# Twenty-one identity products on TensorE in the first tiles, and SyncE's DMA instructions in the order of the listing

## The chip, the cores and the metric

The kernel runs on one core of a Trainium2 chip. Its time is the device time of one execution in microseconds (us). Three executions of the kernel before took 613.67, 614.55 and 615.40 us; the median is 614.55 us.

## What is computed

Attention with a mask from hashed buckets, followed by a gated convolution block. There are 4 batches of 8 heads; each (batch, head) has 768 rows of 64 numbers. Cut to what matters:

```python
q_bits = (np.einsum('bhsd,dk->bhsk', q, proj) > 0)      # 6 sign bits of each row
k_bits = (np.einsum('bhsd,dk->bhsk', k, proj) > 0)
mask = q_bucket[:, :, :, None] == k_bucket[:, :, None, :]
scores = np.where(mask, scale * q @ k.T, -1e9)
attn = softmax(scores)                                  # rows of 768
x = attn @ v                                            # heads side by side: (4, 768, 512)
gate = sigmoid(causal convolution of x over 5 rows, weights conv_w)
out = (gate * (x @ w_val)) @ w_out
```

## The kernel before

**Units and tiles.** A unit is one (batch, head): 32 of them, numbered 0 to 31. A tile is 128 query rows of a unit: 6 per unit, 192 in all, numbered `k`. The main loop runs over `k`. For each tile TensorE makes the scores (`s`, four products, L311), VectorE the row maxima (`nm`, L317) and two small factors (the last is `nb`, L327), ScalarE the exponentials (`p`, L335), GpSimd the division by the row sums (L351), TensorE six transposes (`tp`, L360), ScalarE the copies of them (`pt`, L369). When all six tiles of a unit are transposed, `attn_v` multiplies by the values (`av`, L383) in six steps, two in every iteration with odd `k`. The convolution and the two large products (`pair_x`, `moe`, L445 and L470) are generators that get a step per iteration too, so that they fill TensorE between the tiles of later units. Their results leave through `out_dram<-o` (L480).

**What a unit needs before its first scores.** `prep(i)` prepares unit `i` while unit `i-1` is worked on. It begins in the iteration that starts the scores of unit `i-1` (L562), and goes on one step per iteration (L575). In the order of the listing it
- loads the values `vt` (L181; only for even units, since one load serves two heads). `vt` has two buffers, so the load for unit `i` can't start before `attn_v(i-3)` has read the older buffer for the last time;
- rounds the raw rows `r` to `aq` (GpSimd, L197), and, a step later, makes the remainder `bq` (GpSimd, L200);
- copies halves of them between partitions with four DMAs: `ak<-aq` (L201), `bk<-aq` (L202), `bk<-bq` (L203), `bq<-aq` (L204). The fourth overwrites what the third reads, so it waits until the third has landed;
- puts the bucket rows behind them with two small DMAs, `aq<-u` (L210) and `ak<-u` (L211); for later units they come out of DRAM and are named `ud`;
- loads the raw rows of unit `i+5` (`load_raw`, L212, the DMA is L175).

The scores of unit `i` read `aq`, `ak`, `bq`, `bk`, so they wait for the last of these six DMAs.

**The bucket rows.** `bits(i)` makes them for four units at once, from the raw rows of units `i` to `i+3`: a product of four parts (`m<-r`, L217) and a comparison (L222). The table `marks` (L537) says in which iteration a step runs: for units 8 to 11 the first product is in iteration 34, for units 12 to 15 in iteration 58. The raw rows of unit 11 are loaded by `prep(6)`, those of unit 15 by `prep(10)`. For units 16 and later `early_bits` does the same from rows loaded into `hh` and `hl` (L240).

**The start.** `first_prep` prepares unit 0 without DMAs between partitions. Its product `tp<-r,proj_sb` (L277) and the comparisons from it (L288) come first, then the scores of tile 0. `first_bits` makes the bucket rows of units 0 to 3 by two products L217 in the first iterations.

**What sets the order.** The work is listed under `tc.manual_schedule(engines=ENGINES)` (L522): on each engine in `ENGINES` the instructions stand in the order of the listing. Before, the set holds TensorE (PE), ScalarE (ACT), VectorE (DVE) and GpSimd (POOL). SyncE (SP) is not in it: a scheduler with a cost model set the order of its instructions. SP issues all DMAs but one, and does nothing else. It takes them strictly one after the other: if the next one has to wait for an engine or for a DMA, all behind it stand too.

Of the kernel before, what the change touches and what calls it, by code (L numbers as in the profile page):

```python
# [8 lines left out]
FP32 = mybir.dt.float32  # L9
# [6 lines left out]
I32 = mybir.dt.int32  # L16
U32 = mybir.dt.uint32

ENGINES = {mybir.EngineType.PE, mybir.EngineType.Activation, mybir.EngineType.DVE, mybir.EngineType.Pool}
BIG = float(2.0 ** 60)  # L20
TINY = float(2.0 ** -126)

# [4 lines left out]
def kernel(  # L27
# [10 lines left out]
    nc = tc.nc  # L38
    B, H, _, S = qk.shape
    P = 128  # L40
# [27 lines left out]
    ps_v = ctx.enter_context(tc.tile_pool(name="ps_v", bufs=1, space=PSUM))  # L68
    ps_m = ctx.enter_context(tc.tile_pool(name="ps_m", bufs=1, space=PSUM))

    ident = const.tile([P, P], FP32, name="ident")
# [65 lines left out]
    def load_conv():  # L137
        if conv_w.dtype == mybir.dt.int64:
            w = const.tile([P, NP * KW, 2], I32, name="cw64")
            nc.sync.dma_start(out=w, in_=conv_w.bitcast(I32).rearrange("p (n t) -> p n t", t=2))  # L140
            t = const.tile([P, NP * KW], FP32, name="cwt")
            yield
            a, d = yield from from_float64(w, t)
            yield
            nc.vector.tensor_tensor(out=cw_sb, in0=d, in1=a, op=ALU.add)
        else:
            nc.sync.dma_start(out=cw_sb, in_=conv_w)

    def load_weights():
        parts = [(src[:, c, :], hl[0][:, c, :], hl[1][:, c, :])  # L150
                 for src, hl in ((w_val, wv), (w_out, wo)) for c in range(NP)]
        here = []

        def fetch():
            if len(here) == len(parts):
                return
            src = parts[len(here)][0]
            if src.dtype == mybir.dt.int64:
                w = wst.tile([P, 512, 2], I32, name="w64")
                nc.sync.dma_start(out=w, in_=src.bitcast(I32).rearrange("p (n t) -> p n t", t=2))  # L160
            else:
                w = wst.tile([P, 512], FP32, name="w32")
                nc.sync.dma_start(out=w, in_=src)
            here.append(w)

        fetch()
        for n, (_, hi, lo) in enumerate(parts):
            yield
            yield from split_weight(here[n], hi, lo, fetch)

    def load_raw(i):
        if i < len(units):
            b, h = units[i]
            raws[i] = raw.tile([P, S], FP32, name="r")
            nc.sync.dma_start(out=raws[i], in_=qk[b, h])  # L175

    def load_values(i):
        b, h = units[i]
        if h % 2 == 0:
            vts[i] = vp.tile([P, KB, P], FP32, name="vt")  # L180
            nc.sync.dma_start(out=vts[i], in_=v[b, h // 2])  # L181
        else:
            vts[i] = vts[i - 1]
# [78 lines left out]
    def first_bits():  # L262
        u = stk.tile([P, S], FP32R, name="u", bufs=2)
        for hf in range(2):
            yield
            sl = slice(hf * HS, (hf + 1) * HS)
            signs(u[:, sl], product([raws[jj][:, sl] for jj in range(4)]))
        cur["u"] = u
        load_raw(5)

    def first_prep():

        r = raws[0]
        aq, ak, bq, bk = stacks[0] = [stk.tile([P, S], FP32R, name=nm) for nm in ("aq", "ak", "bq", "bk")]
        z = ps_t.tile([P, 512], FP32, name="tp")
        for g in range(4):
            nc.tensor.matmul(out=z[32 * g:32 * g + 2 * NB, 0:HS], lhsT=proj_sb[:, 2 * NB * (g // 2):2 * NB * (g // 2 + 1)],  # L277
                             rhs=r[:, HS * (g % 2):HS * (g % 2 + 1)], start=True, stop=True, tile_position=(0, 32 * g))
        nc.scalar.copy(out=aq[0:D], in_=r[0:D])
        nc.vector.tensor_copy(out=bk[D:P], in_=r[D:P])  # L280
        nc.vector.tensor_copy(out=ak[0:D], in_=r[D:P])
        nc.gpsimd.tensor_tensor(out=bk[0:D], in0=r[D:P], in1=bk[D:P].bitcast(FP32), op=ALU.subtract)

        def low_part(o, e):
            nc.vector.tensor_tensor(out=bq[D:P, o:e], in0=r[0:D, o:e], in1=aq[0:D, o:e].bitcast(FP32), op=ALU.subtract)  # L285

        def one_hot(g, o, e):
            nc.vector.tensor_scalar(out=(aq, ak)[g // 2][D:M, HS * (g % 2) + o:HS * (g % 2) + e],  # L288
                                    in0=z[32 * g:32 * g + 2 * NB, o:e],
                                    scalar1=rows_sb[32 * g:32 * g + 2 * NB, 2:3],  # L290
                                    scalar2=rows_sb[32 * g:32 * g + 2 * NB, 3:4], op0=ALU.is_ge, op1=ALU.mult)

        one_hot(0, 0, P)
        one_hot(2, 0, HS)
        one_hot(3, 0, HS)
        low_part(0, P)
        one_hot(0, P, HS)
        low_part(P, HS)
        nc.scalar.copy(out=bq[0:D], in_=r[0:D])
        yield  # L300
        one_hot(1, 0, HS)
        low_part(HS, S)

    def scores(k):
        i, qt = tiles[k]
        aq, ak, bq, bk = stacks[i]
        qs = slice(qt * P, (qt + 1) * P)
        s = ss[k] = ps_s.tile([P, 2, 512], FP32, name="s")
        for lq, rk, n in ((aq, ak, M), (bq, bk, P)):
            for hf in range(2):  # L310
                nc.tensor.matmul(out=s[:, hf, 0:HS], lhsT=lq[0:n, qs],  # L311
                                 rhs=rk[0:n, hf * HS:(hf + 1) * HS], start=n == M, stop=n == P)
# [195 lines left out]
    def step(gens):  # L508

        while gens:  # L510
            try:
                return next(gens[0])
            except StopIteration:
                gens.pop(0)
# [6 lines left out]
    N = len(tiles)  # L521
    with tc.manual_schedule(engines=ENGINES):  # L522
        for i in range(5):
            load_raw(i)
        load_values(0)
        rest = first_prep()
        next(rest)
        weights = [[load_weights()], [load_conv()]]
        preps = [first_bits(), prep(1)]
        scores(0)  # L530
        next(preps[1])
        step(preps)
        step(weights[0])
        step(weights[1])
        ahead = [early_bits()]
        near = {i: [bits(i)] for i in (4, 8, 12)}
        marks = {10: near[4], 11: ahead, 16: near[4], 17: ahead, 22: ahead, 28: ahead, 34: near[8], 40: near[8], 46: ahead, 52: ahead,  # L537
                 54: ahead, 56: ahead, 58: near[12], 60: near[12], 62: ahead, 64: ahead}
        for gens in near.values():
            step(gens)  # L540
        for k in range(N + LAG + 1):
            if 0 <= k - LAG - 1:
                keep_transposed(k - LAG - 1)
            pair = k % 2 == 0 and 0 <= k - 2 < N
            if k < N:
                maxima(k)
            if pair:
                row_sums(k - 2)
            if k < N:
                factors(k)  # L550
            if pair:
                recip(k - 2)
            if 0 <= k - 2 < N:
                normalise(k - 2)
            if k < N:
                shifts(k)
            if k == 0:
                finish([rest])
            if k + 1 < N:
                if tiles[k + 1][0] != tiles[k][0]:  # L560
                    finish(preps)
                    preps = [prep(tiles[k + 1][0] + 1)]  # L562
                scores(k + 1)
            if k < N:
                exponentials(k)
            if k - 1 in marks and k - 1 not in (11, 17):
                step(marks[k - 1])
            if k >= 60 or k % 2:
                step(convs)

            thin = k // 6 % 8 in (7, 0) and k < 186
            for _ in range(3 if cur["gates"] else (1, 0)[k % 2] if thin else 1):
                step(moes)
            cur["gates"] = max(0, cur["gates"] - 1)
            step(preps)  # L575
            if k in marks:
                step(marks[k])
            if k in (3, 7, 9, 13, 15):
                step(weights[1])
            if k % 6 != 3 and k > 4:  # L580
                step(weights[0])
            if k % 2:
                step(avs)
                step(avs)
            if 0 <= k - LAG < N:
                transposes(k - LAG)
        accs[:] = [(ps_m, "m"), (ps_t, "tp"), (ps_s, "s"), (ps_t, "tp"), (ps_s, "s")]
        finish(avs)
        cur["gates"] = 0
        cur["end"] = True  # L590
        while convs:
            step(convs)
            step(moes)
        finish(moes)
# [59 lines left out]
```

## Time and profile before

| | |
|---|---|
| median of three executions | 614.55 us (613.67 to 615.40) |
| the profiled execution's own time | 613.79 us |
| its span, first to last instruction | 611.9 us |
| PE busy (matmuls, ends modelled) | 585.5 us, 96% of the span |
| DVE, ACT, POOL busy | 428.8, 420.2, 386.5 us (70%, 69%, 63%) |
| DMA queue of SP | 28832 packets, 63.93 MB, 38.1% of 16 engines' span |

A row of the timeline has start and duration in us, the engine, the line, the operation, the tile written and the tiles read, and how many instructions it stands for; in brackets how long the engine was idle before, and what ended that. `SPq` rows are DMA issues: their duration is the time of issuing, not of the transfer. A row of the waits has the waiting engine and line, what it waited for, then the total in us, how often, and the longest.

### The profile page before, as it was taken

How to read it: one execution, taken by the hardware profiler on the slowest of the kernel's cores; microseconds unless marked ns; L12 is line 12 of the kernel's file. 1: busy time of each engine (PE TensorE's matmuls, PEld its weight loads, DVE VectorE, ACT ScalarE, POOL GpSimd, SP SyncE). 2: the span in 40 equal slices, each digit the busy share in tenths (PEclk: the TensorE clock that was granted, in tenths of full speed). 3: DMA queues.
4: the chain of work that ended last, by engine and by line, in shares of the span. 5: the costliest groups of instructions: out<-in, count | busy, mean ns of one | idle time of the engine just before them, and what ended most of it. 6: DMA issues, size and time to landing. Idle time of an engine off the chain costs nothing.

```text
span 611.9 us, 10670 instructions
## 1 busy us (share of the span) xinstructions
PE 585.5 (96%) x3496; PEld 422.1 (69%) x3496; DVE 428.8 (70%) x1020; ACT 420.2 (69%) x881; POOL 386.5 (63%) x373
## 2 busy tenths in 40 slices
PE   5889999999999999999999999999999999999997
PEld 2656665665567777776667777777768787775995
DVE  6788889898776856587657857578765867565532
ACT  2778888787787766677796767677787676764300
POOL 3566877878656766677655768477745776454321
PEclk9999999999999999999999999999999999999999
DMA  7476566455742342233334323423333123100111
GB/s 231 123 206 198 161 175 177 131 160 148 226 109 81 83 121 70 82 105 86 111 90 123 80 74 89 113 83 92 101 87 90 45 55 100 47 19 1 51 52 51
DMA packets 29030, 64.64 MB, mean 106 GB/s; under 512 B 4936, under 2 KB 10056, under 8 KB 28976
## 3 DMA queue, kind: packets, MB, share of 16 engines
q1 hardware_dynamic: 28832, 63.93, 38.1%
q8 instruction: 28, 0.46, 0.3%
q14 instruction: 26, 0.21, 0.1%
q10 hardware_dynamic: 144, 0.03, 0.0%
HBM read 30.60 MB, written 7.86 MB: 63 GB/s over the span
## 4 chain that ended last, share of the span: by engine, by line
PE 80%; ACT 15%; DVE 3%; issue 1%; DMA 1%; ACTq 0%; DVEq 0%
PE av L383 22%; PE s L311 20%; PE tp L360 16%; PE m L470 8%; PE m L445 7%; ACT p L335 6%; ACT pt L369 5%; ACT x L391 3%; PE m L217 2%; PE tp L445 1%; PE tp L470 1%; PE s L470 1%; PE s L445 1%; DVE nm L317 1%; DMA packed<-in_proj_dram 1%
## 5 line engine op out<-in xcount | busy, mean ns | idle before, releaser
L351 POOL TENSOR_SCALAR p<-p,ri 128x768 f32<-128x768 f32 x192 | 205.4, 1074 | 152.1 <-DVE nb L327 130.9
L317 DVE TENSOR_REDUCE nm<-s 128x1 f32<-128x768 f32 x192 | 182.8, 952 | 72.1 <-PE s L311 71.3
L369 ACT COPY pt<-tp 128x384 f32<-128x384 f32 x384 | 165.9, 485 | 86.0 <-PE tp L360 85.3
L335 ACT ACTIVATE p<-s,nb,gs 128x768 f32<-128x768 f32 x192 | 193.0, 1005 | 29.6 <-DVE nb L327 26.9
L360 PEld LDWEIGHTS tp<-ident,p 128*128 128x128 f32 x1152 | 129.5, 142 | 75.4 <-issue 50.1
L360 PE MATMUL tp<-ident,p 128*128 128x128 f32 x1152 | 164.7, 279 | 2.6 <-ACT pt L369 1.6
L383 PE MATMUL av<-pt,vt 128*64 128x384 f32 x768 | 144.9, 498 | 0.0
L311 PE MATMUL s<-ak,aq 76*128 76x384 f32 x384 | 117.9, 388 | 14.6 <-ACT p L335 12.6
L311 PE MATMUL s<-bk,bq 128*128 128x384 f32 x384 | 101.7, 346 | 0.3 <-DVE bq L285 0.3
L383 PEld LDWEIGHTS av<-pt,vt 128*64 128x64 f32 x768 | 47.0, 136 | 60.5 <-issue 60.4
L311 PEld LDWEIGHTS s<-ak,aq 76*128 76x128 f32 x384 | 59.2, 194 | 28.8 <-ACT p L335 25.2
L414 DVE SCALAR_TENSOR_TENSOR g<-x,cw_sb,g 128x768 f32<-128x768 f32 x64 | 75.9, 1187 | 2.2 <-POOL g L412 2.1
L311 PEld LDWEIGHTS s<-bk,bq 128*128 128x128 f32 x384 | 71.5, 193 | 1.1 <-DVE bq L285 0.8
L456 POOL TENSOR_TENSOR hl<-ht,hh 128x384 fp32r<-128x384 f32 x32 | 32.3, 1009 | 40.0 <-DVE hh L454 40.0
L200 POOL TENSOR_TENSOR bq<-r,aq 128x768 fp32r<-128x768 f32 x31 | 56.8, 1833 | 0.1
L391 ACT COPY x<-av 64x384 f32<-64x384 f32 x64 | 30.4, 475 | 32.1 <-PE av L383 31.5
L404 POOL TENSOR_TENSOR xl<-x,xh 128x384 fp32r<-128x384 f32 x32 | 33.4, 1057 | 17.0 <-DVE xh L403 17.0
L327 DVE TENSOR_SCALAR nb<-nm,gs 128x1 f32<-128x1 f32 x192 | 40.6, 211 | 3.5
L445 PE MATMUL m<-xh,wv 128*128 128x384 f32 x200 | 42.8, 338 | 0.0
L450 DVE TENSOR_TENSOR ht<-m,g 128x384 f32<-128x384 f32 x25 | 13.9, 556 | 37.9 <-PE m L445 33.4
L335 ACT ACTIVATION_READ_ACCUMULATOR p<-s,nb,gs 128x1 f32 x192 | 39.5, 206 | 0.0
L470 PE MATMUL m<-wo,hh 128*128 128x512 f32 x144 | 38.1, 394 | 0.0
(86 smaller groups left out, 477.9 us busy)
## 6 DMA issues: line engine op xcount, KB each, us to landing
r<-in_qk_dram SPq DMA_DIRECT2D x32, 384.0 KB
vt<-in_v_dram SPq DMA_DIRECT2D x16, 384.0 KB
out_dram<-o SPq DMA_DIRECT2D x24, 256.0 KB
ak<-aq SPq DMA_DIRECT2D x31, 192.0 KB
bk<-aq SPq DMA_DIRECT2D x31, 192.0 KB
bk<-bq SPq DMA_DIRECT2D x31, 192.0 KB
bq<-aq SPq DMA_DIRECT2D x31, 192.0 KB
hh<-in_qk_dram SPq DMA_DIRECT2D x16, 192.0 KB
```

What stands on the lines that cost most here:

```text
L200: nc.gpsimd.tensor_tensor(out=bq, in0=r, in1=aq.bitcast(FP32), op=ALU.subtract)
L311: nc.tensor.matmul(out=s[:, hf, 0:HS], lhsT=lq[0:n, qs], rhs=rk[0:n, hf * HS:(hf + 1) * HS], start=n == M, stop=n == P)
L317: nc.vector.tensor_reduce(out=nm, in_=s[:, :, 0:HS], axis=AX.XY, op=ALU.max, negate=True)
L335: nc.scalar.activation(out=p, in_=s[:, :, 0:HS], func=AF.Exp, bias=nb, scale=gs.pop(k), accum_out=sm[:, k % 2, 0:1])
L351: nc.gpsimd.tensor_scalar(out=p, in0=p, scalar1=rcs.pop(k), scalar2=1.0, op0=ALU.mult, op1=ALU.mult)
L360: nc.tensor.transpose(out=tp[:, n * P:(n + 1) * P], in_=p[:, kb * P:(kb + 1) * P], identity=ident)
L369: nc.scalar.copy(out=pt[:, :, qo:qo + P], in_=tp[:, 0:HS].rearrange("p (a b) -> p a b", b=P))
L383: nc.tensor.matmul(out=av[s * D:(s + 1) * D, 0:HS], lhsT=vt[:, kb, hh * D:(hh + 1) * D], rhs=pt[kb // 3][:, kb % 3, :], start=(kb == 0), s ...
L391: nc.scalar.copy(out=x[hh * D:(hh + 1) * D, o:o + HS], in_=av[s * D:(s + 1) * D, 0:HS])
L414: nc.vector.scalar_tensor_tensor(out=g, in0=x[:, k:k + S], scalar=w, in1=g, op0=ALU.mult, op1=ALU.add)
L445: nc.tensor.matmul(out=acc[:, 0:HS], lhsT=wv[wi][:, c, j * P:(j + 1) * P], rhs=xs_[(c, o)][xi], start=(m == 0), stop=(m == 11))
L470: nc.tensor.matmul(out=acc, lhsT=hs[(o, j)][hi][:, tb * P:(tb + 1) * P], rhs=wo[wi][:, j, :], start=(m == 0), stop=(m == 11))
```

## The change

Two things. `ENGINES` gets SyncE, so that SP's DMA instructions stand in the order of the listing, as those of the other engines do. And a helper `spin(n)` lists `n` products of the identity with itself into a buffer of the pool `ps_v` whose content nobody reads; it is called four times: with 7 ahead of `first_prep`, with 4 behind its product, and with 5 in iterations 1 and 2.

```diff
--- before.py
+++ after.py
@@ -16,7 +16,8 @@
 I32 = mybir.dt.int32
 U32 = mybir.dt.uint32
 
-ENGINES = {mybir.EngineType.PE, mybir.EngineType.Activation, mybir.EngineType.DVE, mybir.EngineType.Pool}
+ENGINES = {mybir.EngineType.PE, mybir.EngineType.Activation, mybir.EngineType.DVE, mybir.EngineType.Pool,
+           mybir.EngineType.SP}
 BIG = float(2.0 ** 60)
 TINY = float(2.0 ** -126)
 
@@ -268,6 +269,12 @@
         cur["u"] = u
         load_raw(5)
 
+    def spin(n):
+
+        z = ps_v.tile([P, 512], FP32, name="av")
+        for _ in range(n):
+            nc.tensor.matmul(out=z[:, 0:P], lhsT=ident, rhs=ident, start=True, stop=True)
+
     def first_prep():
 
         r = raws[0]
@@ -276,6 +283,7 @@
         for g in range(4):
             nc.tensor.matmul(out=z[32 * g:32 * g + 2 * NB, 0:HS], lhsT=proj_sb[:, 2 * NB * (g // 2):2 * NB * (g // 2 + 1)],
                              rhs=r[:, HS * (g % 2):HS * (g % 2 + 1)], start=True, stop=True, tile_position=(0, 32 * g))
+        spin(4)
         nc.scalar.copy(out=aq[0:D], in_=r[0:D])
         nc.vector.tensor_copy(out=bk[D:P], in_=r[D:P])
         nc.vector.tensor_copy(out=ak[0:D], in_=r[D:P])
@@ -523,6 +531,7 @@
         for i in range(5):
             load_raw(i)
         load_values(0)
+        spin(7)
         rest = first_prep()
         next(rest)
         weights = [[load_weights()], [load_conv()]]
@@ -573,6 +582,8 @@
                 step(moes)
             cur["gates"] = max(0, cur["gates"] - 1)
             step(preps)
+            if k in (1, 2):
+                spin(5)
             if k in marks:
                 step(marks[k])
             if k in (3, 7, 9, 13, 15):
```

Lines of the changed kernel have higher numbers (L181 becomes L182, L201 to L204 become L202 to L205, L311 becomes L319). ACT, DVE and POOL keep their rows; PE gains the four groups.

PE in the changed kernel, in iterations 0 to 2 (`s` are the scores of tiles 2 to 4, `m<-r` the two products of `first_bits`, `av<-ident` a product of `spin`):

```order
L218 MATMUL m<-r,proj_sb 32x384 x4
L319 MATMUL s<-ak,aq 128x384 x2
L319 MATMUL s<-bk,bq 128x384 x2
L218 MATMUL m<-r,proj_sb 32x384 x4
L276 MATMUL av<-ident 128x128 x5
L319 MATMUL s<-ak,aq 128x384 x2
L319 MATMUL s<-bk,bq 128x384 x2
L276 MATMUL av<-ident 128x128 x5
```

Before, the same rows stand there without `av<-ident`. The two groups stand ahead of the scores of tiles 3 and 4; the other two, of 7 and 4, stand ahead of `tp<-r,proj_sb` and between it and the scores of tile 0.

SP at the preparation of unit 6, before; in brackets the semaphores that a DMA waits for (`PE_49` is TensorE's, `Pool_49` GpSimd's, `DMAHW` with a number one of eight that earlier DMAs raise when they land):

```order
L201 DMA ak<-aq 64x768 [waits DMAHW7_49,Pool_49]
L202 DMA bk<-aq 64x768 [waits DMAHW0_49]
L203 DMA bk<-bq 64x768 [waits DMAHW1_49,Pool_49]
L175 DMA r<-in_qk_dram 128x768 [waits DMAHW2_49]
L181 DMA vt<-in_v_dram 128x768 [waits DMAHW3_49,PE_49]
L204 DMA bq<-aq 64x768 [waits DMAHW4_49,DMAHW1_49]
L210 DMA aq<-u 12x768 [waits DMAHW7_49,DMAHW5_49,DMAHW0_49]
L160 DMA w_1328<-in_w_out_dram 128x1024 [waits DMAHW6_49]
L240 DMA hl<-in_qk_dram 128x384
L211 DMA ak<-u 12x768 [waits PE_49]
```

The same place in the changed kernel:

```order
L182 DMA vt<-in_v_dram 128x768 [waits DMAHW5_49,PE_49]
L202 DMA ak<-aq 64x768 [waits DMAHW6_49,Pool_49]
L203 DMA bk<-aq 64x768 [waits DMAHW7_49]
L204 DMA bk<-bq 64x768 [waits DMAHW0_49,Pool_49]
L205 DMA bq<-aq 64x768 [waits DMAHW1_49,DMAHW0_49]
L211 DMA aq<-u 12x768 [waits DMAHW7_49,DMAHW6_49,DMAHW2_49]
L212 DMA ak<-u 12x768 [waits DMAHW3_49]
L176 DMA r<-in_qk_dram 128x768 [waits DMAHW4_49]
L161 DMA w_1353<-in_w_out_dram 128x1024 [waits DMAHW5_49]
```

The load of `vt`, with its wait for PE, moved from the fifth place of the group to the first, and the load of `r` from the fourth to the last of the unit; `ak<-u`, which stood among the rows of an earlier unit (the `ak<-u` of the last row before belongs to unit 7), now stands behind `aq<-u` of its own.

SP at the preparation of unit 4 in the changed kernel, where four loads `hl` stand between `vt` and the copies:

```order
L161 DMA w_673<-in_w_val_dram 128x1024 [waits DMAHW5_49,DVE_49]
L182 DMA vt<-in_v_dram 128x768 [waits PE_49]
L241 DMA hl<-in_qk_dram 128x384 x2
L241 DMA hl<-in_qk_dram 128x384 [waits DMAHW1_49]
L241 DMA hl<-in_qk_dram 128x384 [waits DMAHW2_49]
L202 DMA ak<-aq 64x768 [waits DMAHW3_49,Pool_49]
```

Before, those `hl` stood ahead of the group of unit 4, and `vt` in its middle, behind `aq<-u`, as it does for unit 6 behind `r`.

## The prediction

> **What bounds the kernel now.** First the page: the busy share of PE (busy, instructions), the clock that it shows per slice, and the chain that ended last.
>
> ```profile
> PE 585.5 (96%) x3496; PEld 422.1 (69%) x3496; DVE 428.8 (70%) x1020; ACT 420.2 (69%) x881; POOL 386.5 (63%) x373
> PEclk9999999999999999999999999999999999999999
> PE 80%; ACT 15%; DVE 3%; issue 1%; DMA 1%; ACTq 0%; DVEq 0%
> ```
>
> PE sets the time: 80% of the chain is its own work, in the order of the listing. So whatever PE saves or waits for comes off or on the end almost in full, and DMAs have 1% of the chain: no transfer is late now. Next the waits of SP's queue (what SP stood for; total us, times, longest):
>
> ```profile
> SPq L204 <- DMA bk<-bq: 26.1, 27, 2.4
> ...
> SPq L181 <- PE av L383: 2.6, 4, 1.3
> ```
>
> SP takes its DMAs one by one, so what it waits for holds up all that is behind. For the landing of `bk<-bq` it waits once per unit; for `vt` (L181) hardly at all, since that load stands far enough back in the group of its unit. The change alters just that.
>
> **First part: the identity products.** The chain in the first 44 us (start, us, what; each row is PE's pieces of one kind):
>
> ```profile
> 13.08 1.65 PE s L311 x4
> 14.73 1.53 PE m L217 x8
> ...
> 19.50 1.65 PE s L311 x4
> 21.15 1.28 PE tp L360 x6
> ...
> 24.84 0.72 PE s L311 x4
> ...
> 37.63 0.78 PE m L217 x8
> 38.41 0.81 PE tp L360 x6
> ...
> 43.78 0.96 PE s L311 x4
> ```
>
> The same work takes 1.65, 1.53 and 1.28 us at first, and 0.96, 0.78 and 0.81 later: PE runs at little more than half speed at the start. The page's clock row shows nothing of it. PE works without a gap from 19.50 on and is fast from 24.84, some 5 us later; 3.2 us without a gap from 13.08 weren't enough.
>
> What fits: L217 shows 8 instructions for its 4 products, so an fp32 product is two passes. A pass of 128 columns takes 1.28 / 6 = 0.21 us slow and 0.81 / 6 = 0.135 us fast (the transposes; estimate), so a spin product takes about 0.43 us slow, 0.27 fast. The identity is ready at 1.3 us:
>
> ```profile
> 1.01 0.29 POOL masks.py:199 TENSOR_SCALAR_AFFINE_SELECT ident<-ident 128x128 f32<-128x128 f32 x1
> 14.92 0.21 DVE L327 TENSOR_SCALAR nb<-nm,gs 128x1 f32<-128x1 f32 x1
> 16.29 0.68 DVE L222 TENSOR_SCALAR u<-m,packed 128x384 fp32r<-128x384 f32 x1 [1.16 <-PE m L217]
> ```
>
> Seven products (3.0 us) fill 1.3 to 4.3, in which PE waits. The 4 behind (1.7 us) stretch into the scores of tile 0 by some 0.4 us; those wait for DVE's comparisons anyway, and cost nothing. So PE is dense from 1.3 us on, and I take it to be fast by 13 us. Then scores and product in the chain end at 13.08 + 0.96 + 0.78 = 14.8 instead of 16.26, and L222, which waited 1.16 us for them, starts when DVE is through with L327, at 15.15: 1.14 us earlier. The next pair, scores and transposes, saves (1.65 + 1.28) - (0.96 + 0.81) = 1.16 us. Behind it the tiles go at the pace of ACT and DVE as later ones do. The groups of 5 take 1.35 us each when fast: the first lies ahead of scores that wait for ACT until 16.36, the second ends at 16.36 + 0.96 + 1.35 = 18.7, where the next scores could start at 19.50 - 1.14 = 18.4: 0.3 us in the way. Sum: 1.14 + 1.16 - 0.3 = 2.0; I take **-1.8**. Bounds: the four chain rows save 1.65 + 1.53 + 1.65 + 1.28 - 0.96 - 0.78 - 0.96 - 0.81 = 2.6 at most, and if PE is still slow, two groups of 2.15 us and the scores between them end at 16.26 + 4.3 + 1.65 = 22.2, 2.7 us behind the 19.50 at which the next scores start now. So -2.6 to +2.7.
>
> **Second part: SP in the order of the listing.** Unit 6 shows it. SP, then PE (timeline of before):
>
> ```profile
> 88.35 0.50 SPq L201 DMA_DIRECT2D ak<-aq  x1
> 88.90 0.59 SPq L202 DMA_DIRECT2D bk<-aq  x1
> 91.03 0.46 SPq L203 DMA_DIRECT2D bk<-bq  x1
> ...
> 92.51 0.33 SPq L181 DMA_DIRECT2D vt<-in_v_dram  x1
> 93.64 0.47 SPq L204 DMA_DIRECT2D bq<-aq  x1
> 94.21 0.79 SPq L210 DMA_DIRECT2D aq<-u  x1
> 95.05 0.49 SPq L160 DMA_DIRECT2D w<-in_w_out_dram  x1
> ```
>
> ```profile
> 90.96 1.51 PE L383 MATMUL av<-pt,vt 128*64 128x384 f32 x8
> ...
> 99.28 0.85 PE L217 MATMUL m<-r,proj_sb 128*32 128x384 f32 x8
> ```
>
> The last `av` of unit 3 ends at 90.96 + 1.51 = 92.47, and `vt` goes out at 92.51: it waited for that, as the listing says. Before, `ak<-aq`, `bk<-aq`, `bk<-bq` and the load of `r` had gone out by then. Now all of them stand behind `vt`. With T for the end of that `av`: `vt` at T, `ak<-aq` at T+0.5, `bk<-aq` 0.55 later, `bk<-bq` 0.6 later (T+1.65), then the wait for its landing (91.03 to 93.64: 2.6) and `bq<-aq` at T+4.25, `aq<-u` 0.57 later, `ak<-u` 0.84 later (94.21 to 95.05: T+5.65), `r` another 0.84 later: **T+6.5**. Queued behind `r` are only weights, `hh` and `hl`, which have some us to spare except at unit 4.
>
> How long a raw load takes, from the first one (SP's issue, ACT's first use):
>
> ```profile
> 0.74 2.29 SPq L175 DMA_DIRECT2D r<-in_qk_dram  x5
> 4.15 0.83 ACT L279 CAST aq<-r 64x768 fp32r<-64x768 f32 x1 [1.70 <-DMA r<-in_qk_dram]
> ```
>
> 3.4 us, so `r` of unit 11 lands at T+9.9. The product that reads it stands at 99.28 = T+6.8. **PE waits 3.1 us** there. The same holds at unit 10:
>
> ```profile
> 153.08 1.51 PE L383 MATMUL av<-pt,vt 128*64 128x384 f32 x8
> ...
> 161.38 0.85 PE L217 MATMUL m<-r,proj_sb 128*32 128x384 f32 x8
> ```
>
> 161.38 - 154.59 = 6.8 again: two times 3.1 = **6.2 us**. The scores right behind these products then find their rows there.
>
> At the other units the scores are the first to wait. `ak<-u` lands at T+5.65+2.6 = T+8.25 if it takes as long as `bk<-bq`. For 14 even units, 4 to 30, `vt` has to wait; the time from T to the first scores is shortest at unit 18 and longest at unit 30:
>
> ```profile
> 292.63 1.51 PE L383 MATMUL av<-pt,vt 128*64 128x384 f32 x8
> 301.92 0.62 PE L311 MATMUL s<-ak,aq 76*128 76x384 f32 x2 [0.24 <-ACT p L335]
> 505.77 0.81 PE L383 MATMUL av<-pt,vt 128*64 128x384 f32 x4
> 515.71 0.59 PE L311 MATMUL s<-ak,aq 76*128 76x384 f32 x2
> ```
>
> 7.8 and 9.1 us, in the middle 8.45: just in time while the queue is empty. It isn't: `vt` and three copies are in flight. The second view has SP's waits for the landing of `bk<-bq` at 26.1 / 27 = 1.0 us on average (the rest of the 2.6 went into issues between) and 2.4 at the longest: a full queue adds up to 1.4 us. So each of the 11 units (without 4, 6 and 10) is late by 0 to 8.25 + 1.4 - 8.45 = 1.2 us. I take a third of that, nearer to the average than to the longest wait: 11 x 0.4 = **4.4 us** (0 to 13.2).
>
> Unit 4 has four loads `hl` between `vt` and its copies:
>
> ```profile
> 47.78 2.03 SPq L240 DMA_DIRECT2D hl<-in_qk_dram  x4
> 60.09 1.51 PE L383 MATMUL av<-pt,vt 128*64 128x384 f32 x8
> 69.83 0.59 PE L311 MATMUL s<-ak,aq 76*128 76x384 f32 x2
> ```
>
> They take 2.1 us to issue, so `ak<-u` lands at T+10.35; the scores stand at 69.83 - 61.60 = T+8.2: 2.1 us late, up to 1.4 more in the queue, and as much again where later loads stand behind. I take **4.0** (2.1 to 4.9).
>
> In before PE stood for 1.5 us at the longest behind the first microseconds:
>
> ```profile
> PE s L311 <- ACT p L335: 12.6, 31, 1.5
> ```
>
> So no row shows whether waits of 3 or 4 us throw it back to slow; it is a rival below. The Trainium skill speaks against the change here: "TensorE: Matmul & The Clock Gate", section "HAM oscillation — how this bites in real kernels", has the clock fall back to half rate after an idle window of about 3.4 us. By that the wait at unit 4 would cost some 2 us more, the two of 3.1 us nothing, and the sum would be that much higher; no run here shows it yet.
>
> The rest of the reordering (results, `ud`, weights) I cost at nothing: PE's work of the tiles between issue and use hides it. If that cover fails, it adds to the wait at unit 4, where most is queued.
>
> Sum: 6.2 + 4.4 + 4.0 = 14.6; the two parts together 14.6 - 1.8 = **+12.8 us**. Against the profiled execution's 613.79 us (span 611.9), that is **626.6 us**; the median of the runs shown, 614.55, is 0.8 above that execution.
>
> **Rivals.** (1) The transfers are still in time, and only the clock counts: 613.8 - 1.8 = **612.0**. It decides if `vt` may go out 3.1 us or more ahead of T, for instance because it waits for an earlier step of `attn_v`. Against it: in before, SP waits for PE `av` there, and 92.51 follows 92.47. Chance 0.06. (2) The smaller waits stay hidden, and ACT, which has 15% of the chain, makes up 2 us while PE stands: 613.8 + 6.2 + 2.1 - 2 - 1.8 = **618.3**. For it: 8.45 over 8.25. Chance 0.20; a fifth of it goes to ACT making up so much that the whole stays within 0.3%. (3) The early products don't make PE fast: 613.8 + 14.6 + 2.7 = **631.1**. For it: the 3.2 us from 13.08 that weren't enough. Chance 0.12. (4) Each of the three long waits throws PE back to slow until it was dense for 5 us again, as from 19.50 on: 5 x (1 - 0.96 / 1.65) = 2.1 us each, 626.6 + 6.3 = **632.9**. For it: the slow start. Against it: 31 short waits that did nothing. Chance 0.08.
>
> **How the numbers follow.** The forecast has 0.54, the rivals 0.06, 0.20, 0.12, 0.08. A run can tell about 0.3%, 1.8 us, from no change. Faster by more: rival 1, 0.06. Within: the fifth of rival 2, 0.04. Slower by more: 0.90. The lowest sum of bounds outside rival 1 is 613.8 + 8.3 - 2 - 2.6 = 617.5, and the highest 613.8 + 6.2 + 13.2 + 4.9 + 2.7 = 640.8; eleven waits won't all meet the fullest queue, and I cut at 637. From 617 to 637 lie nine tenths of the forecast's cases, rivals 3 and 4, and most of rival 2: about 8 in 10.
>
> **What would show it.** SP's rows at every even unit: `vt` right behind an `av`, then the copies within 2 us. PE waits for DMA `r` at L218 twice, about 3 us each, near 98 and 165 us; waits for `aq`, `ak` or `bq` at L319 at even units only; the largest loss between 60 and 75 us. Scores in some 1.0 us instead of 1.65 before 20 us. If the waits of PE still name no DMA, the second part is wrong; if the scores near 16 us still take 1.65, the first is.

## The result, and the profile after

The changed kernel takes **659.89 us** (median of five executions, 657.41 to 661.34) against 614.55 us for the kernel before on the same chip: ratio 1.073, 95% interval 1.0703 to 1.0756. It is 45.3 us slower; 12.8 were forecast, and the time lies above the range of 617 to 637. The profiled execution took 661.34 us, its span is 659.5.

The page of the changed kernel, the rows that were shown of before: busy time (share, instructions), TensorE's clock by slice, the chain that ended last.

```profile
PE 606.2 (92%) x3538; PEld 432.8 (66%) x3538; DVE 426.8 (65%) x1020; ACT 419.6 (64%) x881; POOL 383.2 (58%) x373
PEclk9999797997979999998979999998999999999999
PE 64%; DMA 13%; ACT 9%; DVE 7%; SPq 3%; issue 2%; POOL 1%; POOLq 0%; ACTq 0%; DVEq 0%
```

Two things have come into the chain: transfers (1% before, 13% now) and SP's queue. And PE is busy 20.7 us longer; the clock row, all nines before, has seven slices with a 7 or an 8, so part of PE's work ran slow. SP's waits (total us, times, longest):

```profile
SPq L182 <- PE av L391: 152.0, 14, 16.0
SPq L205 <- DMA bk<-bq: 99.9, 31, 4.9
```

Before, the first was 2.6 us in 4 waits, the second 26.1 in 27. SP now stands for `attn_v` once in each of 14 even units, and for `bk<-bq` 3.2 us each time instead of 1.0. What PE and ACT wait for in turn:

```profile
PE s L319 <- DMA ak<-ud: 11.2, 6, 2.6
PE m L218 <- DMA r<-in_qk_dram: 9.0, 2, 4.8
PE s L319 <- DMA ak<-u: 7.3, 3, 4.6
ACT m L112 <- DMA w<-in_w_val_dram: 7.2, 1, 7.2
ACT m L112 <- DMA w<-in_w_out_dram: 4.4, 1, 4.4
```

None of these five stood in the profile before. The last two are ACT's, for a load of weights (`w`) that stands on SP's queue behind a unit's group; the prediction put those loads at nothing.

Unit 6 shows the chain of it (SP, then PE at the bucket product of units 8 to 11):

```profile
96.97 0.33 SPq L182 DMA_DIRECT2D vt<-in_v_dram  x1
97.39 0.53 SPq L202 DMA_DIRECT2D ak<-aq  x1
97.97 0.59 SPq L203 DMA_DIRECT2D bk<-aq  x1
98.65 0.54 SPq L204 DMA_DIRECT2D bk<-bq  x1
103.18 0.46 SPq L205 DMA_DIRECT2D bq<-aq  x1
105.41 0.49 SPq L176 DMA_DIRECT2D r<-in_qk_dram  x1
```

```profile
95.42 1.51 PE L391 MATMUL av<-pt,vt 128*64 128x384 f32 x8
...
108.79 1.49 PE L218 MATMUL m<-r,proj_sb 128*32 128x384 f32 x2 [4.21 <-DMA r<-in_qk_dram]
```

The last `av` of unit 3 ends at T = 95.42 + 1.51 = 96.93, and `vt` goes out at 96.97: the order is as forecast, and so is the place of `bk<-bq`, T+1.7 (T+1.65 forecast). But `bq<-aq` follows 4.5 us after `bk<-bq`, not 2.6. The 384 KB of `vt` are in the queue ahead of that copy, so it lands 1.9 us later, and all behind it goes out 1.9 us later: `r` at T+8.5 instead of T+6.5. PE waits 4.2 us instead of 3.1. The rest of the product then takes 1.49 us, where all eight passes took 0.85 before: the clock granted from 107.55 to 114.38 us is 0.50.

### The profile page after: what moved, and what is told of

It reads as the page before. It is cut to its first block, busy times and chain, and to the rows that moved or that the text cites. A ratio compares the mean times of both kernels' runs of the same rounds, so it can differ in the third digit from the quotient of the medians.

```text
span 659.5 us, 10727 instructions
## 1 busy us (share of the span) xinstructions
PE 606.2 (92%) x3538; PEld 432.8 (66%) x3538; DVE 426.8 (65%) x1020; ACT 419.6 (64%) x881; POOL 383.2 (58%) x373
## 4 chain that ended last, share of the span: by engine, by line
PE 64%; DMA 13%; ACT 9%; DVE 7%; SPq 3%; issue 2%; POOL 1%; POOLq 0%; ACTq 0%; DVEq 0%
PE av L391 18%; PE s L319 15%; PE tp L368 12%; DMA bk<-bq 8%; PE m L478 7%; PE m L453 5%; ACT p L343 4%; ACT pt L377 3%; DVE nm L325 2%; DMA ak<-ud 2%; ACT x L399 2%; PE m L218 1%; PE tp L453 1%; PE tp L478 1%; SPq L211 1%
## 5 line engine op out<-in xcount | busy, mean ns | idle before, releaser
L359 POOL TENSOR_SCALAR p<-p,ri 128x768 f32<-128x768 f32 x192 | 202.1, 1057 | 201.1 <-DVE nb L335 169.9
L368 PE MATMUL tp<-ident,p 128*128 128x128 f32 x1152 | 166.7, 282 | 4.0 <-ACT pt L377 3.0
L391 PE MATMUL av<-pt,vt 128*64 128x384 f32 x768 | 152.4, 520 | 0.0
L319 PE MATMUL s<-ak,aq 76*128 76x384 f32 x384 | 118.4, 389 | 33.5 <-ACT p L343 12.6
L319 PE MATMUL s<-bk,bq 128*128 128x384 f32 x384 | 101.5, 346 | 1.2 <-DVE bq L293 1.2
L391 PEld LDWEIGHTS av<-pt,vt 128*64 128x64 f32 x768 | 48.7, 141 | 64.2 <-issue 64.1
L319 PEld LDWEIGHTS s<-ak,aq 76*128 76x128 f32 x384 | 59.5, 195 | 46.9 <-ACT p L343 32.7
L422 DVE SCALAR_TENSOR_TENSOR g<-x,cw_sb,g 128x768 f32<-128x768 f32 x64 | 72.1, 1126 | 2.2 <-POOL g L420 2.1
L319 PEld LDWEIGHTS s<-bk,bq 128*128 128x128 f32 x384 | 71.8, 194 | 1.8 <-DVE bq L293 1.2
L201 POOL TENSOR_TENSOR bq<-r,aq 128x768 fp32r<-128x768 f32 x31 | 56.7, 1829 | 0.1
```

The costliest lines, as they stand in the source:

```text
L201: nc.gpsimd.tensor_tensor(out=bq, in0=r, in1=aq.bitcast(FP32), op=ALU.subtract)
L319: nc.tensor.matmul(out=s[:, hf, 0:HS], lhsT=lq[0:n, qs], rhs=rk[0:n, hf * HS:(hf + 1) * HS], start=n == M, stop=n == P)
L359: nc.gpsimd.tensor_scalar(out=p, in0=p, scalar1=rcs.pop(k), scalar2=1.0, op0=ALU.mult, op1=ALU.mult)
L368: nc.tensor.transpose(out=tp[:, n * P:(n + 1) * P], in_=p[:, kb * P:(kb + 1) * P], identity=ident)
L391: nc.tensor.matmul(out=av[s * D:(s + 1) * D, 0:HS], lhsT=vt[:, kb, hh * D:(hh + 1) * D], rhs=pt[kb // 3][:, kb % 3, :], start=(kb == 0), s ...
L422: nc.vector.scalar_tensor_tensor(out=g, in0=x[:, k:k + S], scalar=w, in1=g, op0=ALU.mult, op1=ALU.add)
```

## Where the time went, by units

The row of a unit's first scores stands in the timeline of every run. Its start, less the start in before, is what the run has lost up to there; the differences between units tell where. In us, from the profiled executions (the columns behind "after" are runs of the next section):

| up to the first scores of unit | forecast | after | order only | products in long waits | wait first, data last | values last |
|---|---|---|---|---|---|---|
| 3 | -1.8 | -2.5 | 0.4 | -0.2 | 0.2 | 1.6 |
| 5 (from 3) | 4.0 | 6.9 | 7.2 | 8.3 | 8.6 | 0.0 |
| 6 | 3.1 | 6.2 | 6.5 | 4.4 | 3.7 | 2.5 |
| 9 (from 6) | 0.4 | 7.3 | 5.1 | 4.9 | 7.4 | 0.0 |
| 10 | 3.1 | 6.8 | 5.7 | 5.6 | 4.8 | 1.1 |
| 31 (from 10) | 4.0 | 22.9 | 13.7 | 13.7 | 3.2 | 0.0 |
| sum | 12.8 | 47.8 | 38.7 | 36.7 | 27.9 | 5.2 |

## The experiments

"Before" on the same chip took 613.9 to 614.4 us in all of them.

### The two parts apart

Products alone: SP taken out of `ENGINES` again. Order alone: `ENGINES` with SP, no `spin`.

```diff
-ENGINES = {PE, Activation, DVE, Pool, SP}
+ENGINES = {PE, Activation, DVE, Pool}
```

> The identity products alone; SyncE's order is again the scheduler's. Theory A (the loss is SyncE's order, the products bring the 2.8 us by which unit 1 starts earlier in the changed kernel): 614.5 - 2.8 = 611.8 us, no stretch of slow clock behind 5 us. Rival B (the products themselves, or the early full clock, cost something later): above 616 us, and slow stretches of the clock in the profile.

> SyncE in the order of the listing alone, without the identity products. Theory A: the whole loss stays and the 2.8 us of the start are missing: 659.9 + 2.8 = 662.7 us, with as many slow stretches of the clock (7, give or take 1). Rival B (the two parts need each other): clearly under 655 us.

Products alone: 612.53 us, ratio 0.9986 (0.9968 to 1.0005). Order alone: 654.86 us, ratio 1.0677 (1.0651 to 1.0704). So the order makes the loss. That the order alone is 5 us faster than both parts together was not expected; most of it goes with the clock (below): its profiled execution has three half-clock stretches, 17 us in all, where the changed kernel has seven, 41 us. The products win less than expected, and windows of TensorE's work show why (from:to, us, PE busy, ..., granted clock, DMA share, GB/s). Products alone:

```profile
3.64:11.25 7.61, 5.63 (x34) 3.29 (x36) 6.77 (x10) 1.67 (x3) 4.76 (x3) 1.00 1.01 366
11.25:18.08 6.83, 6.06 (x29) 3.38 (x22) 5.45 (x15) 2.16 (x4) 0.00 (x0) 0.50 0.97 254
```

The clock is full from 4.4 us on, the first that the trace gives, but falls back to half at 11.25, as PE is idle for 2.0 of the 7.6 us ahead, while DVE makes the comparisons of unit 0. In the changed kernel's profiled execution, with the same products at the same places, it stayed at full. That was luck: of the nine profiled runs with these twenty-one products the other eight all fall back between 10.4 and 13.3 us. Over the nine, unit 1's scores start between 0.05 us later and 2.8 us earlier.

The page of this run also gives a measure for the changed kernel:

```profile
PE 587.9 (96%) x3538; PEld 425.6 (70%) x3538; DVE 429.6 (70%) x1020; ACT 419.3 (69%) x881; POOL 384.9 (63%) x373
```

The same 3538 passes take 606.2 us there: 18.3 us more. Most of it is the half clock: PE was busy for 34.2 us in the seven stretches at half, and half of that is 17.1 us, less 3.0 us for the one stretch of this run.

### The values last

```diff
-        load_values(i)
         r = raws[i]
...
         load_raw(i + 5)
+        load_values(i)
```

> The changed kernel with the load of the values moved in the listing from the first to the last place of a unit's preparation, behind the load of the raw rows. Theory A (the wait of that load holds up the unit's six copies, and the rest follows from it): the loss is gone, 610 to 614 us, PE waits for no DMA, no slow stretches. Rival C (the rest of the listing's order, ak<-u and r late and in the program's places, costs by itself): 620 us or more, with PE waiting for ak<-u or r.

Measured: 615.59 us, ratio 1.0027 (1.0012 to 1.0043), a little above the range expected. So one load of 384 KB at the head of every second unit's group carries nearly the whole loss. What is left in its profile: PE's waits for `r`, and SP's rows at unit 6.

```profile
PE m L218 <- DMA r<-in_qk_dram: 2.0, 2, 1.7
```

```profile
87.93 1.88 SPq L241 DMA_DIRECT2D hl<-in_qk_dram  x4
...
92.63 0.46 SPq L203 DMA_DIRECT2D bk<-bq  x1
98.17 0.46 SPq L204 DMA_DIRECT2D bq<-aq  x1
```

Here no `vt` stands ahead, but four `hl` of 192 KB each: `bq<-aq` follows 5.5 us after `bk<-bq`. So it isn't `vt` as such that makes the copy late, but bytes ahead of it. (The profiled execution, 618.84 us, is the slowest of this run's nine, so the 5.2 us in the table are more than its median shows.)

### Wait first, data last

This separates the two things that the load of `vt` does at the head of the group: SP's wait for `attn_v` stays, with a sixth of the data; five sixths go behind the load of `r`.

```diff
-            nc.sync.dma_start(out=vts[i], in_=v[b, h // 2])
+            nc.sync.dma_start(out=vts[i][:, 0:1], in_=v[b, h // 2, :, 0:1])
...
         load_raw(i + 5)
+        load_rest(i)      # vts[i][:, 1:KB], for even units
```

> The changed kernel, but the load of vt is cut in two: a sixth (64 KB) stays at the head of the unit's DMAs and keeps the wait for attn_v there; the other five sixths (320 KB) go behind the load of r. Theory D (the wait at the head costs what the prediction's steps say, and what was missed is that the copy bk<-bq has to land behind the 384 KB of vt in the same queue, some 1.9 us later at each even unit): bk<-bq lands within about 3 us again at even units, PE waits about 3 us at each of the two late bucket products, hardly at the other even units, unit 4 keeps its 4 to 7 us because the four hl are still ahead; 626 to 633 us. Theory W (the wait itself holds up the chain by this much, whatever lies in the queue): PE waits 4 to 5 us at the two products and 1.4 to 2.6 at the other even units as before; 650 to 660 us.

Measured: 640.32 us, ratio 1.0426 (1.0397 to 1.0456): between the two theories, 20 us under the changed kernel. SP's waits, its rows at unit 6, and PE's waits:

```profile
SPq L182 <- PE av L397: 150.1, 14, 15.3
SPq L210 <- DMA bk<-bq: 82.5, 31, 5.3
```

```profile
101.29 0.33 SPq L182 DMA_DIRECT2D vt<-in_v_dram  x1
...
102.97 0.55 SPq L209 DMA_DIRECT2D bk<-bq  x1
106.24 0.46 SPq L210 DMA_DIRECT2D bq<-aq  x1
...
108.46 0.49 SPq L176 DMA_DIRECT2D r<-in_qk_dram  x1
```

```profile
PE m L224 <- DMA r<-in_qk_dram: 5.4, 2, 2.7
...
PE s L325 <- DMA ak<-u: 5.1, 1, 5.1
```

SP stands for `attn_v` as often and as long as in the changed kernel (150 us), but `bq<-aq` follows 3.3 us after `bk<-bq` instead of 4.5, `r` goes out at T+7.2, and PE waits 2.7 us for it at both products. Behind unit 10 only 3.2 us are lost, where the forecast had 4.0 and the changed kernel has 22.9. So for the ordinary even units the wait at the head costs what the prediction said, and the rest comes with the data ahead of the copies: later landings, and the half clock behind the waits for them. What stays too large is units 4 and 5 (8.6) and 7 to 9 (7.4). The chain of this run there (start, us, what):

```profile
73.58 0.49 SPq L176
...
74.59 6.32 DMA w<-in_w_val_dram
...
80.99 0.09 ACT m L112
```

The load of `w`, 512 KB, is issued behind the late `r`; ACT takes its instructions in order and stands for it; PE's transposes and scores stand behind ACT's copies and exponentials. The same row stands in the chain of the changed kernel, between units 8 and 9:

```profile
144.26 5.47 DMA w<-in_w_out_dram
...
149.81 0.09 ACT m L112
...
152.27 1.65 PE s L319 x4
```

### The four raw rows behind the weights

On top of the last run: the four loads `hl` (768 KB) are taken out of unit 4's group.

```diff
-        marks = {10: near[4], 11: ahead, 16: near[4], 17: ahead, 22: ahead, ...
+        marks = {10: near[4], 11: ahead, 16: near[4], 21: ahead, 22: ahead, ...
```

> The run with the wait first and the data last, with the four loads hl taken out of unit 4's group: they go out behind the load of w that follows it. Theory H (these 768 KB ahead of unit 4's copies and of w hold up both, so that PE waits for ak<-u and ACT for w): PE's wait of 5.1 us for ak<-u at unit 4 and ACT's wait of 9.2 us for w go, units 4 and 5 lose at most 2 us together instead of 8.8, and the time is 631 to 635 us. Rival (SP's wait for attn_v at the head is enough to make both late): 637 us or more.

Measured: 640.02 us, ratio 1.0424: no gain over 640.32, against the expectation. Half of the theory holds:

```profile
ACT m L112 <- DMA w<-in_w_val_dram: 7.0, 2, 5.0
...
PE s L325 <- DMA ak<-u: 0.5, 1, 0.5
```

PE's wait at unit 4 went from 5.1 to 0.5 us, and unit 4 loses 0.7 instead of 5.3. But ACT still stands 5.0 us for `w`, and unit 5 loses 4.6. At unit 4 two waits lie side by side; with one gone the other is late next. Taking away ACT's wait alone was not tried: the buffers for `w` are two, and its steps share an accumulator with the bucket products.

### Products in the waits

To price the clock: identity products ahead of the scores and products that wait, so that PE isn't idle there. The first run puts 15 at unit 4 and at the two late bucket products and 6 at each other even unit from 6 on; the second has only those of unit 4, of the late products, and 4 each at units 18, 20, 26 and 28; the third puts 15 and 10 into the long waits of the run with the data last.

```diff
     def scores(k):
+        if qt == 0 and i in (4, 18, 20, 26, 28):
+            warm(s[:, 0, 0:P], 15 if i == 4 else 4)
...
-            z = product([raws[i + jj][:, sl] for jj in range(4)])
+            z = product([raws[i + jj][:, sl] for jj in range(4)], 15 if hf == 0 and i > 4 else 0)
```

> The changed kernel with more identity products where PE waits: 15 ahead of the scores of unit 4 and of the two late bucket products, 6 ahead of the first scores of every other even unit from 6 on, into the tiles that the real products then overwrite. They take 0.27 us each at full clock, less than the waits there. Theory D (of the 47.6 us that the span grew by, the 41 us at half clock cost some 12 to 18, and come from the waits): no slow stretch is left, and 642 to 648 us. Rival E (PE would have waited anyway, the slow clock costs little): 655 us or more. Transfers alone, late as they are, would give the rest.

> The changed kernel with 15 identity products ahead of the first scores of unit 4 and ahead of each of the two late bucket products, and 4 ahead of the first scores of units 18, 20, 26 and 28: they fill the waits after which the clock was at half, and are shorter than these. No order of a DMA changes. Theory C (beside the waits themselves, some 31 us in the trace of the changed kernel, the half clock behind them costs the rest, about 17 us): no half-clock stretch is left behind 20 us, PE busy without the added products falls by some 15 us, and the time is 643 to 648 us. Theory E (the half clock is covered by ACT's and DVE's pace; the waits are what counts): 655 to 661 us.

> The run with the wait first and the data last (640 us), with 15 identity products ahead of the first scores of unit 4 and 10 ahead of each late bucket product. Theory C (the half clock behind the long waits is paid for on top of them; in that run's record it holds for 17 us behind 20 us): no half-clock stretch is left at units 4, 6 and 10, and 4 to 8 us are gained: 632 to 636 us. Theory E (it is covered by ACT and DVE): 639 us or more.

First: 651.75 us, ratio 1.0613 (1.0591 to 1.0634), 8 us under the changed kernel, 4 above what the one theory expected and 3 under the other. Second: 649.98 us, ratio 1.0574 (1.0537 to 1.0610), 10 us under it, 2 above what the clock theory expected and 5 under the other. Third: 643.82 us, ratio 1.0487 (1.0471 to 1.0503), 3.5 us slower than without the products, so the theory of the clock missed here. Half-clock stretches stayed at 81 and 153 us, where PE stands for ACT and ACT for `w`, and no product had been put there. The products won 2.9 us at units 7 to 9, but the stretch at 81 us lasts 6.8 us instead of 3.4, and a new one at 330 us goes with 3.4 us lost at units 18 and 19 (0.8 without products). Why these two came is not settled.

So two runs with most of the half clock gone are 8 to 10 us faster, and a third gains nothing; the added products alone don't give a firm price. There is another measure, the clock granted in every execution beside its time:

| | time in us, and granted clock |
|---|---|
| changed kernel | 661.34 at 0.969, 659.89 at 0.971, 660.18 at 0.973, 658.61 at 0.974, 657.41 at 0.977 |
| order alone | 657.24 at 0.978, 655.10 at 0.979, 654.61 at 0.981, 652.31 at 0.987 |

A straight line through either row falls by 4.7 us per 0.01 of clock, and both lines come to 646 to 647 us at a clock of 1.000. By this estimate, which reaches beyond the clocks measured, **some 13 of the 45 us** go with the half clock, and so do 4 of the 5 us between the two kernels. Time and clock are only seen together here. An execution with longer waits would show more half clock too, so that the clock alone costs 13 us is not shown.

The clock's part in the units behind 10 can be read from the stretch from 200 to 600 us (columns as above): the changed kernel, the order alone, the second run of this group.

```profile
200.00:600.00 400.00, 381.11 (x2253) 280.80 (x2254) 252.88 (x625) 277.42 (x583) 243.99 (x233) 0.98 0.31 80
```

```profile
200.00:600.00 400.00, 383.02 (x2306) 283.66 (x2306) 261.40 (x635) 282.62 (x594) 250.08 (x238) 1.00 0.30 81
```

```profile
200.00:600.00 400.00, 386.28 (x2333) 286.79 (x2333) 258.69 (x629) 281.70 (x592) 249.63 (x238) 1.00 0.30 79
```

In 400 us the changed kernel gets through 53 passes fewer than the order alone, at a clock of 0.98. Behind unit 10 the two runs at 1.00 lose 13.7 us each, the changed kernel 22.9. By these two, **10.5 us** (13.7 - 3.2) are the price of the data ahead of the copies with a full clock, and 9.2 us go with the clock; of these the half clock can make at most 6.8 directly (three stretches of 3.4, 6.8 and 3.4 us, shown in the last section), and the rest is open. Nor is 13.7 a fixed price: the first run of this group, with products ahead of every even unit and one half-clock stretch of 3.4 us there, loses 18.1 us behind unit 10. The order alone has no products there, so its full clock isn't the products' doing. It had such waits too:

```profile
PE s L312 <- DMA ak<-ud: 6.1, 4, 2.6
```

Whether a wait of 2 to 2.6 us brings the clock down changes from run to run.

### Rows early, and more products

`r` between `bk<-bq` and `bq<-aq`, where SP stands anyway, and `vt` at the end of the unit's group:

```diff
         nc.sync.dma_start(out=bk[D:P].bitcast(FP32), in_=bq[D:P].bitcast(FP32))
+        load_raw(i + 5)
         nc.sync.dma_start(out=bq[D:P].bitcast(FP32), in_=aq[0:D].bitcast(FP32))
...
-        load_raw(i + 5)
+        load_values(i)
```

> The changed kernel with the load of r moved between bk<-bq and bq<-aq, where SP stands for the landing of bk<-bq anyway, and the load of vt moved to the end of the unit's DMAs. If the rest of the loss of the run with the values last was r behind that landing (2.5 and 1.1 us at the two late bucket products), nothing of PE's waits for DMAs is left behind 20 us, and the time is that of the products alone or a little less: 611 to 613 us. If r in this place delays bq<-aq and the bucket rows behind it, scores wait at even or odd units: 615 us or more.

> The run with rows early (SP in the order of the listing, r between bk<-bq and bq<-aq, vt at the end of the unit), without the products. If that listing of SP costs nothing, and the wide spread of the run with rows early (613.4 to 618.4) comes from a clock that the products raise early and gaps of PE let fall again, the time is 613.5 to 614.5 us, with runs within 2.5 us of one another. If the listing itself costs something in the first units (conv weights behind a 512 KB load), it is 615 us or more, as with the products.

> The run with rows early, and seven more identity products in gaps of PE: 3 between the two pairs of score products of tile 1, 4 behind the first bucket product of iteration 0. If the clock fell back to half between 11 and 18 us in the run with the products alone because PE was idle too much between 6 and 13 us, it stays at full from about 5 us on, unit 1's scores start 2.5 to 2.8 us earlier than before, and the time is 610 to 611.5 us. If not, unit 1's scores start about 1 us earlier and the time is 612 to 614 us.

> The run with rows early and more products, with the small load of the convolution weights moved from behind a 512 KB load of w to behind the first load of vt. In that run ACT stood 1.8 us for it near 20 us, with TensorE's clock at full all the time. If that wait took back what the full clock had won, unit 1's scores start 2.5 to 2.8 us earlier than before instead of 1.0, and the time is 610.5 to 612.5 us, under both kernels. If not, 613 to 616 us as in that run.

> The kernel before with SP's order as before, the twenty-one products of the change, and the seven more of the run with more products (3 between the two pairs of score products of tile 1, 4 behind the first bucket product of iteration 0). If the products alone won only about 1 us because the clock fell back to half between 11 and 18 us, it now stays at full behind 7 us, unit 1's scores start 2 to 2.8 us earlier than before, and the time is 611 to 612 us, under the kernel before and the run with the products alone. If DMAs of unit 1 bound the start instead, the clock is at full and unit 1's scores start at most 1.2 us earlier: 612.5 to 614 us.

With rows early: 615.22 us, ratio 1.0019 (0.9999 to 1.0039). In its trace (of 613.39 us, the fastest of its ten executions) no unit from 2 to 31 loses more than 0.1 us: the loss of the reordering is gone from there on. Without products: 615.36 us, ratio 1.0015 (1.0003 to 1.0028), so the remaining 1 us and the spread (613.96 to 618.54) are not the products'. Its rows name one cause, in the first tiles:

```profile
ACT cwt L92 <- DMA cw<-in_conv_w_dram: 2.3, 1, 2.3
```

The listing puts the small convolution weights behind a 512 KB load of `w`. With seven more products in gaps of PE (rows early, more products): 615.68 us, ratio 1.0028 (1.0006 to 1.0051), above both ranges expected, though the clock of its trace stays at full from 4.6 us to the end; with the convolution weights ahead of `w` as well: 613.99 us, ratio 1.0002 (0.9992 to 1.0012), not the 610.5 to 612.5 expected. In its trace PE then stands 3.3 us for `ak<-u` of unit 1: another DMA is late next.

More products in the order of before: **612.59 us, ratio 0.9979 (0.9967 to 0.9992)**. This beats the kernel before by 0.2%, but not the twenty-one products alone (612.53 us, ratio 0.9986): the seven more won nothing that these times show. The clock in this run, and the wait that is left:

```profile
11.25:18.08 6.83, 6.51 (x51) 4.73 (x44) 6.26 (x16) 3.18 (x6) 1.09 (x2) 1.00 0.98 249
...
25.00:32.00 7.00, 5.83 (x30) 5.13 (x28) 6.83 (x20) 4.97 (x11) 4.39 (x4) 0.76 0.59 186
```

```profile
23.29 0.59 PE L320 MATMUL s<-ak,aq 76*128 76x384 f32 x2 [1.71 <-DMA ak<-u]
```

The seven more products hold the clock at full through the stretch in which it fell before, but unit 1's scores come only 1.3 us earlier: PE is there before their bucket rows have landed. The transfers of unit 1 are the next bound of the start, not TensorE. And behind that wait of 1.71 us the clock does fall, against the expectation: to half at 24.95 us, for 3.4 us (0.76 over the second window).

## Why the prediction was wrong in size, step by step

**Products, -1.8.** The profiled execution gave -2.5, with the scores at 16 us in 1.0 us as foretold; that it came so near is luck, since its clock is the only one of nine that didn't fall back. Alone they gave 1.4 us by the times (interval: 2.0 faster to 0.3 slower). The step "PE is dense from 1.3 us on" is wrong: PE idles between 6 and 13 us, and the clock falls again in eight of nine traces.

**`vt` waits for `attn_v`, and all behind it stands.** Right: 14 waits at even units from 4 on, and `vt` within 0.1 us of the end of `av`. Rival 1 (transfers still in time) is out.

**The two late products, 6.2.** Right in place and kind. Their waits are 4.2 and 4.8 us instead of 3.1. With the data behind, both are 2.7. Mis-sized: the landing of `bk<-bq`, taken as 2.6 us, is 4.5. Units 6 and 10 lost 13.1 us together; 9.0 of it are the two waits, and behind both the clock was at half for 6.8 us.

**Eleven other even units, 4.4.** This is the step that failed most. "A full queue adds up to 1.4 us, I take a third" was drawn from the waits of before, where `vt` stood *behind* `bk<-bq`; no row of before shows that copy landing behind 384 KB. Units 11 to 31 lost 22.9 us instead of 4.0. With the data behind they lost 3.2, as the step says for an emptier queue; with it ahead and a full clock 13.7 in two runs, 18.1 in a third.

**Unit 4, 4.0.** Units 4 and 5 lost 6.9 us. PE's wait for `ak<-u` was 4.6 us, inside the bounds (2.1 to 4.9). The rest came from the half clock behind it (70.00 to 76.83 us): the scores of unit 4 and the `av` after them took 1.62 and 2.76 us instead of 0.98 and 1.46.

**"The rest of the reordering I cost at nothing".** Wrong for `w`. The named cover, "PE's work of the tiles between issue and use", doesn't help where ACT itself is the engine that stands. ACT's wait of 4.4 us lies on the chain, between units 8 and 9; that of 7.2 us, at unit 4, runs beside PE's wait for `ak<-u` and is not on it. Units 7 to 9 lost 7.3 us, where 0.4 was forecast. How much of that is ACT's wait and how much the half clock, the runs don't separate fully: with products at the even units, and no half clock there, 2.8 us stayed.

**Rival 4, the half clock (0.08, +6.3).** Its mechanism is real, and its price was too low: three falls of 2.1 us each were supposed, and there are seven. At some 8 to 13 us, it should have stood in the forecast. The reason given against it, "31 short waits that did nothing", only covers waits up to 1.5 us.

## What to carry to other kernels

On a queue that issues in order, a load with a late wait costs twice: its wait holds up what is behind it, and then its bytes land ahead of the small copies that everybody needs. Put the loads with slack last in the group, and price a copy by what is in the queue ahead of it, in bytes, not by how it landed where the queue held something else. And a wait of TensorE is not paid by its own length alone: from about 1.7 us on the clock behind it may, but need not, be at half for 3 to 7 us (it fell behind waits of 1.7 to 2.6 us, and stayed at full behind others of 1.9 to 2.6).

## What the runs showed of the hardware that was not expected

**The clock falls before a whole window is idle.** Pairs of windows of the changed kernel, ahead of and behind four falls:

```profile
66.59:70.00 3.41, 1.01 (x10) 0.64 (x6) 1.37 (x4) 2.10 (x6) 2.97 (x4) 1.00 0.20 45
70.00:76.83 6.83, 4.68 (x14) 2.28 (x15) 1.41 (x5) 0.51 (x1) 1.56 (x2) 0.50 0.79 231
...
298.70:302.11 3.41, 1.48 (x11) 1.10 (x9) 1.98 (x4) 2.03 (x6) 2.73 (x3) 1.00 0.77 194
302.11:305.52 3.41, 3.41 (x12) 1.32 (x12) 2.32 (x6) 0.00 (x0) 1.81 (x2) 0.50 0.54 116
332.83:336.24 3.41, 1.43 (x11) 1.15 (x9) 2.25 (x4) 3.40 (x8) 3.41 (x4) 1.00 0.43 87
336.24:343.07 6.83, 6.21 (x20) 3.81 (x21) 2.32 (x6) 0.80 (x2) 3.56 (x3) 0.50 0.49 150
448.89:452.30 3.41, 1.37 (x10) 1.16 (x9) 2.08 (x4) 2.14 (x6) 3.41 (x4) 1.00 0.70 195
452.30:455.71 3.41, 3.41 (x12) 0.98 (x11) 2.32 (x6) 0.00 (x0) 1.67 (x2) 0.50 0.54 115
```

PE was busy for 1.0 to 1.5 of the 3.41 us ahead of each fall, thus idle for 1.9 to 2.4. The Trainium skill, "TensorE: Matmul & The Clock Gate", section "HAM oscillation — how this bites in real kernels", warns of idle gaps above some 3.4 us; the trace doesn't agree: the last three falls go with waits of PE for `ak<-ud` of 1.9, 2.6 and 2.0 us.

**The same products keep the clock in one run and lose it in another.** The twenty-one products gave a start with the clock at full from 5 us on in the changed kernel, and a fall at 11 us with the products alone. Of nine traces with them eight fall between 10.4 and 13.3 us; of the three with seven more products none falls before 24 us, two at 25 and 27 us, behind waits of 1.7 and 3.3 us. The same page, section "Part 1: The HAM clock gate", has a window that runs freely and doesn't start with the kernel; the stretches of 3.41 and 6.83 us fit that.

**A copy lands the later, the more bytes are in the queue ahead of it.** From the issue of `bk<-bq` to that of `bq<-aq`: 2.6 us in before, 3.3 behind 64 KB, 4.5 behind 384 KB, 5.5 behind 768 KB.
